# Talking-heads attention on one core: the last 64 keys of the V product in quarters of the array

## The chip, the cores and the metric

One core of one Trainium2 chip. The metric is device time of the whole kernel in microseconds (us): median of the runs. Engines are named as in the profile: PE is TensorE (matmuls), PEld its weight loads, DVE is VectorE, ACT ScalarE, POOL GpSimd, SP SyncE, which issues most transfers.

## The reference

Four batches, 12 heads, 448 positions, head size 64, all float32:

```python
scores = (q @ k.T) / 8                            # per head
scores = einsum('bhij,hg->bgij', scores, w_pre)   # mix heads
attn = exp(scores - max);  attn = attn / (sum(attn) + 1e-9)
attn = einsum('bhij,hg->bgij', attn, w_post)      # mix heads again
x = attn @ v                                      # the V product, (4*448) x 768
```

Two feed-forward layers follow (768 to 2048 to 768 with ELU, 768 to 1024 to 768 with SoLU and a layer norm). The change is in the attention part alone.

## The kernel before

**Work units.** A group is 10 query rows of a batch with all 12 heads. Two groups make a unit, 90 units in all. A chunk is up to 12 groups (120 query rows) of one batch; there are 17 chunks, whose widths add up to 4 x 448 rows. Ten groups' scores lie on partitions as (row, head), so that a head mix is a matmul.

**Stages.** Per chunk, `add_score` (L446) forms the scores of two heads at a time, four 64x64 quarters of the array at once, into two banks of the ring `sc`, which has three; ACT or DVE evacuate them (L452) and a DMA deals them out into the layout (row, head). Per unit, `pre` (L518, tile `pm`) mixes heads, DVE takes the row maximum (L523), ACT the exponential with its sum (L528), DVE and POOL make `wr`, the weights of the second mix divided by the sum. `post` (L551, tile `po`) then multiplies: stationary is a block of 64 keys of `e` (60 partitions x 64 keys), moving is `wr` (60 x 60: 12 heads x 5 rows), so that keys come out on partitions. A unit has two groups (s) of two halves (r, 5 rows each); each quarter of the array has its own (s, x), x being the half of the partitions on which the keys land. 448 keys are 7 blocks of 64: blocks 2q and 2q+1 for q = 0 to 2 fill both halves of 128 partitions, block 6 is the one left over. In `po` its r = 0 rows lie on the lower half and its r = 1 rows on the upper half, the rest of these columns are zeros, set once at the start (L479). `take` (L559) copies each group's `po` (128 x 480) into the chunk's `at` on ACT or DVE. There are two `po` banks, one per group, and both are needed by each unit: a unit's `post` waits for the `take`s of the unit before.

**The V product** (`mm`, L595 to 601, tile `av`) takes a chunk's `at` when all its groups are in: for each half n of the heads (6 heads), 3 head pairs, 4 key pairs q and the two heads k of the pair, 24 matmuls of 128 partitions x 64 stationary columns, two side by side in the array. For q = 3 the array's 128 rows hold block 6 twice (the host's `vt` has it twice), and the zeros in `at` make each row count once. A half is one bank of `sc`, is copied to SBUF (L607) and stored.

A float32 matmul shows as two instructions in the trace, each with a weight load of its own.

**What sets the order.** Nothing is issued in program order here: every stage is an `op` with a rank (a due time in us), resources and planned costs, and `schedule()` (L298) walks them once at build time: it takes the engine that can start first and of its ready operations the one with the lowest rank. `bufs` (L286) holds the rings, among them 3 `sc`, 3 `pm`, 2 `po`. Each engine then runs the order that came out. The ranks come from L363 to 396 with the planned costs `PRE, POST, AV, SC` (L364); a chunk's two V products are due three units after its last `post`.

Of the kernel before, what the change touches and what calls it, by code (L numbers as in the profile page):

```python
# [9 lines left out]
F32 = mybir.dt.float32  # L10
# [54 lines left out]
def kernel(ctx: ExitStack, tc: tile.TileContext, qa, kt, vt, wpre, wpost,  # L65
# [297 lines left out]
    t_pre, t_post, t_av, t_sc = {}, {}, {}, {}  # L363
    PRE, POST, AV, SC, HID = .76, .83, 2.6, .76, 3.64  # L364
    t, nf, t_hid = T0, 0, None
# [10 lines left out]
    for u in range(NU):  # L376
        while nf < min(NU, u + LEAD + 1):
            plan_front()
        t_post[u] = t
        t += POST  # L380
        if pending and u - pending[0][0] == 3:
            for k in pending.pop(0)[1]:
                t_av[k] = t
                t += AV
        for c in range(NC):
            if last_of[c] == u:
                pending.append((u, [(c, 0), (c, 1)]))
        if u + 1 == NU:
            t_hid = t
            t += 2 * HID  # L390
            for i, k in enumerate(sum((k for _, k in pending), [])):
                t_av[k] = t_hid - 1 + i
# [5 lines left out]
    kt_t, kb, q_t, qb_, sp_t, sp_op, pre_op, e_t = {}, {}, {}, {}, {}, {}, {}, {}  # L398
    po_t, ps_t, st_t, wr_t, v_t, x_t, at_t, T = {}, {}, {}, {}, {}, {}, {}, {}
    k_op, q_op, av_op, sc_ev = {}, {}, {}, {}  # L400
# [76 lines left out]

    for t in po_p:
        op(T0 + 2, lambda e, t=t: nc.vector.memset(t, 0.0), dve=.49)  # L479
    o_clear = {c + 3: clear(sp_t[c][:, CH[c][2]:], .38 * (NH - CH[c][2]), 4.0 + c) for c in range(2)}  # L480
# [24 lines left out]
    for u, sl in enumerate(units):  # L505
# [36 lines left out]
        def post(e, u=u, ns=2):  # L542


            ps = po_t[u] = po_p
            for todo in [[(r, 2 * q + x, q, x) for x in range(2)] for r in range(2) for q in range(3)] + [[(0, 6, 3, 0), (1, 6, 3, 1)]]:
                for r, n, q, x in todo:
                    for s in range(ns):
                        sl = slice(64 * s, 64 * s + 60)
                        out = ps[s][64 * x:64 * x + 64, q * 120:q * 120 + 120].rearrange("p (g a) -> p g a", a=10)  # L550
                        nc.tensor.matmul(out[:, :, 5 * r:5 * r + 5], e_t[u, r][sl, 64 * n:64 * n + 64],  # L551
                                         wr_t[u][sl, r].rearrange("p (g a) -> p g a", a=5), start=True, stop=True)

        def take(e, s, u=u, sl=sl):
            c, g = sl[s]
            if c not in at_t:
                at_t[c] = pools["at"].tile([128, 4, NH, WMAX], F32, tag="at", name="at")
            o, n = 10 * g, min(10, width_of(c) - 10 * g)
            copier(e)(at_t[c].rearrange("p q h r -> p (q h) r")[:, :, o:o + n],  # L559
                      po_t[u][s][:, :480].rearrange("p (x a) -> p x a", a=10)[:, :, :n])  # L560

# [11 lines left out]
        for s, (c, g) in enumerate(sl):  # L573
            at_ops[c].append(op(r0 + 1.2 + .1 * s, lambda e, s=s, take=take: take(e, s), [o], [at_b[c]] if g == 0 else [],
                                [pob[s]] + ([at_b[c]] if g else []), act=.45, dve=.57))


    for c in range(NC):
        b = CH[c][0]
        w = width_of(c)  # L580
        if c == HEAD[b]:
# [7 lines left out]
            for i in range(6):  # L589
                ov.append(op(t_av[c, 0] - VD + 4 * i if b else T0 + 8 + 2.5 * i, lambda e, i=i, load=load: load(e, i), [o_begin], [] if i else [vb], [vb] if i else [], sp=.5, lag=4.0))  # L590
        for n in range(2):
            r = t_av[c, n]
            xb, avb = Buf("x"), Buf("sc")

            def mm(e, c=c, n=n, w=w):  # L595
                ps = x_t[c, n] = ps_sc.tile([128, 512], F32, tag="sc", name="av")[:, :3 * w].rearrange("p (k w) -> p k w", k=3)
                for i in range(3):
                    for q in range(4):
                        for k in range(2):
                            nc.tensor.matmul(ps[64 * k:64 * k + 64, i, :], v_t[CH[c][0]][:, 6 * n + 2 * i + k, q, :], at_t[c][:, q, 6 * n + 2 * i + k, :w],  # L600
                                             start=q == 0, stop=q == 3)

            o = op(r, mm, at_ops[c] + ov, [avb], [vb, at_b[c]], pe=AV * w / 120)

            def take(e, c=c, n=n, w=w):
                T["x", c, n] = pools["xt"].tile([128, 3, WMAX], F32, tag="x", name="x")
                copier(e)(T["x", c, n][:, :, :w], x_t[c, n])  # L607

# [4 lines left out]

            o = op(r + AV + .2, take, [o], [xb], [avb], act=.36, dve=.42)
            T["xs", c, n] = op(r + AV + 1, store, [o], [], [xb], sp=.5, more=.2)

# [62 lines left out]
    gln_t = None  # L679
    lc = NC - 1  # L680
    t0 = t_pre[first[lc]]
# [39 lines left out]
    for ft in range(2):  # L721
        o = None
        for p in range(3):
            o = op(t_hid + HD + ft * .01, lambda e, ft=ft, p=p: hid(0, 0, ft, range(2 * p, 2 * p + 2)),
                   need + [o] + [sc_ev[lc, h] for h in range(NH)], pe=HID / 3)
    for i in range(3):
# [253 lines left out]
```

## Time and profile before

| | us |
|---|---|
| median of 3 runs | 1081.91 |
| the runs | 1080.24, 1081.91, 1084.91 |
| span of the profiled execution, first to last instruction | 1077.6 |
| of this, the attention part up to the first matmul of the feed-forward alone | about 358 |

The total of the profiled execution is not listed apart from the three runs; its span stands 4.3 us below their median. Lines of a profile read: start or group, engine, line of the kernel, operation, written tile <- read tiles, shape, count.

### The profile page before, as it was taken

What the parts mean: (1) busy time and instruction counts of PE and PEld (TensorE: products, weight loads), DVE (VectorE), ACT (ScalarE), POOL (GpSimd) and SP (SyncE); (2) the same over time, 40 slices, a digit from 0 to 9 for tenths busy, and PEclk for the clock granted to TensorE, in tenths of its full rate; (3) what the DMA queues carried; (4) which work ended last, traced back from release to release, by engine and by line L of the source; (5) the groups of instructions that cost most, each with busy time, mean ns of one, the idle gap of its engine ahead of it and who ended that gap; (6) DMA issues with size and microseconds to landing.
All of it is one profiled execution on the core that took longest, in us unless ns stands there. A gap on an engine that the chain in (4) does not pass through costs nothing.

```text
span 1077.6 us, 28434 instructions
## 1 busy us (share of the span) xinstructions
PE 1052.9 (98%) x11800; PEld 886.6 (82%) x11800; DVE 719.2 (67%) x1394; ACT 502.4 (47%) x1068; POOL 240.7 (22%) x240
## 2 busy tenths in 40 slices
PE   6899999999999999999999999999999999999998
PEld 2467777677677889998998999999998889898988
DVE  5587776877878566887878887778754734353522
ACT  3476766776776454333433334333331524242422
POOL 4011111111114324353443443433431000000000
PEclk9999999999999999999999999999999999999999
DMA  6776876776746342415161332424272400000001
GB/s 206 205 225 186 238 229 195 230 229 196 227 146 195 98 147 79 155 52 185 58 204 65 123 117 87 148 78 145 71 273 100 163 23 23 23 28 17 30 15 45
DMA packets 80522, 141.69 MB, mean 131 GB/s; under 512 B 20648, under 2 KB 60424, under 8 KB 80392
## 3 DMA queue, kind: packets, MB, share of 16 engines
q1 hardware_dynamic: 78255, 136.45, 39.9%
q10 hardware_dynamic: 2137, 3.41, 1.1%
q8 instruction: 93, 1.52, 0.6%
q14 instruction: 37, 0.30, 0.1%
HBM read 75.96 MB, written 25.17 MB: 94 GB/s over the span
## 4 chain that ended last, share of the span: by engine, by line
PE 78%; DVE 9%; DMA 6%; ACT 3%; issue 3%; SPq 1%; POOL 1%; ACTq 0%; DVEq 0%; POOLq 0%
PE h L258 15%; PE o L753 15%; PE o L896 11%; PE h L849 11%; PE av L600 6%; PE po L551 6%; PE pm L518 6%; PE sc L446 6%; DMA ws<-in_wo_dram 2%; DVE x L769 1%; DMA sp<-sev 1%; DVE wy L186 1%; DMA ws<-in_wi_dram 1%; PE tr L880 1%; DVE wq L182 1%
## 5 line engine op out<-in xcount | busy, mean ns | idle before, releaser
L753 PE MATMUL o<-gh,woh 128*128 128x448 f32 x384 | 141.3, 368 | 3.6 <-ACT x L767 1.9
L528 ACT ACTIVATE e<-pm,st 128x448 f32<-128x448 f32 x180 | 113.6, 636 | 64.1 <-DVE st L523 56.7
L523 DVE TENSOR_REDUCE st<-pm 128x1 f32<-128x448 f32 x180 | 105.6, 617 | 52.6 <-PE pm L518 50.5
L753 PE MATMUL o<-glo,woh 128*128 128x448 f32 x384 | 140.0, 365 | 0.0
L753 PE MATMUL o<-gh,wol 128*128 128x448 f32 x384 | 139.7, 364 | 0.0
L271 POOL TENSOR_TENSOR glo<-g,gh 128x448 fp32r<-128x448 f32 x64 | 84.0, 1312 | 217.8 <-issue 125.1
L551 PEld LDWEIGHTS po<-wr,e 60*64 60x64 f32 x5040 | 100.8, 135 | 36.2 <-issue 21.7
L446 PE MATMUL sc<-kt,q 64*64 64x448 f32 x816 | 119.5, 560 | 8.9 <-DMA kt<-in_kt_dram 4.0
L896 PE MATMUL o<-w,lh 128*128 128x384 f32 x448 | 120.3, 340 | 0.0
L518 PE MATMUL pm<-sp,wpre_t 64*64 64x448 f32 x720 | 108.6, 556 | 5.0 <-ACT e L528 4.2
L551 PE MATMUL po<-wr,e 60*64 60x60 f32 x5040 | 107.1, 219 | 2.7 <-issue 1.8
L849 PE MATMUL h<-w,x2h 128*128 128x512 f32 x336 | 107.7, 395 | 0.0
L769 DVE TENSOR_TENSOR x<-x,o 128x448 f32<-128x448 f32 x168 | 101.4, 610 | 7.9 <-PE o L753 7.9
L258 PE MATMUL h<-xh,wih 128*128 128x448 f32 x288 | 105.6, 367 | 0.0
L258 PE MATMUL h<-xh,wil 128*128 128x448 f32 x288 | 105.1, 365 | 0.0
L258 PE MATMUL h<-xl,wih 128*128 128x448 f32 x288 | 104.8, 364 | 0.0
L266 ACT ACTIVATE t<-t 128x448 f32<-128x448 f32 x64 | 37.0, 578 | 136.1 <-DVE t L265 136.1
L539 POOL TENSOR_TENSOR wr<-wpost_t,st 128x120 f32<-128x120 f32 x88 | 34.1, 388 | 283.8 <-DVE st L535 228.0
L600 PEld LDWEIGHTS av<-at,v 128*64 128x64 f32 x1632 | 75.5, 137 | 15.9 <-issue 6.5
L600 PE MATMUL av<-at,v 128*64 128x120 f32 (+5 forms) x1632 | 82.9, 258 | 1.3 <-issue 0.8
L896 PEld LDWEIGHTS o<-w,lh 128*128 128x128 f32 x448 | 81.7, 188 | 0.6
L753 PEld LDWEIGHTS o<-gh,woh 128*128 128x128 f32 x384 | 72.1, 188 | 11.9 <-DVE x L769 3.9
(96 smaller groups left out, 1936.3 us busy)
## 6 DMA issues: line engine op xcount, KB each, us to landing
sp<-sev SPq DMA_DIRECT2D x93, 210.0 KB
ws<-in_wi_dram SPq DMA_DIRECT2D x33, 512.0 KB
ws<-in_wo_dram SPq DMA_DIRECT2D x21, 512.0 KB
q<-in_qa_dram SPq DMA_DIRECT2D x34, 192.0 KB
v<-in_vt_dram SPq DMA_DIRECT2D x24, 256.0 KB
w2s<-ws SPq DMA_DIRECT2D x12, 512.0 KB
ws<-in_wo_dram SPq DMA_DIRECT2D x16, 384.0 KB
w2s<-ws SPq DMA_DIRECT2D x16, 384.0 KB
```

What stands on the lines that cost most here:

```text
L258: nc.tensor.matmul(ps[:, :S], a[:, kc * FG + ft * 128:kc * FG + (ft + 1) * 128], x[:, kc, :], start=kc == 0 and n == 0, stop=kc == ECH - 1 ...
L271: nc.gpsimd.tensor_tensor(glo, g, f(gh), ALU.subtract)
L446: nc.tensor.matmul(T[key][i][64 * x:64 * x + 64, :S], q[sl, h % 6 // 2, 64 * x:64 * x + 64], k[sl, :], start=True, stop=True)
L518: nc.tensor.matmul(ps_t[u][r][64 * s:64 * s + 64, :S], wpre_t[p, :], sp_t[c][p, g, :], start=True, stop=True)
L523: nc.vector.tensor_reduce(out=st_t[u][:P, r:r + 1], in_=ps_t[u][r][:P, :S], op=ALU.max, axis=AX.X, negate=True)
L528: nc.scalar.activation(out=t[:P], in_=ps_t[u][r][:P, :S], func=AF.Exp, bias=st[:P, r:r + 1], scale=1.0, accum_out=st[:P, 2 + r:3 + r])
L551: nc.tensor.matmul(out[:, :, 5 * r:5 * r + 5], e_t[u, r][sl, 64 * n:64 * n + 64], wr_t[u][sl, r].rearrange("p (g a) -> p g a", a=5), start ...
L600: nc.tensor.matmul(ps[64 * k:64 * k + 64, i, :], v_t[CH[c][0]][:, 6 * n + 2 * i + k, q, :], at_t[c][:, q, 6 * n + 2 * i + k, :w], start=q ...
L753: nc.tensor.matmul(ps[:, :S], a[:, ft * DM + e * 128:ft * DM + (e + 1) * 128], x, start=n == 0, stop=n == 5)
L769: nc.vector.tensor_tensor(x1[tb][:, e, :], x1[tb][:, e, :], ps[:, :S], ALU.add)
L849: nc.tensor.matmul(ps[:, hf * 512:hf * 512 + 512], a[:, k, :], w, start=n == 0, stop=n == 3 * ECH - 1)
L896: nc.tensor.matmul(ps[:, :384], a[:, k, :], w, start=n == 0, stop=n == 3 * FC - 1)
```

## The change

- `post` now spreads block 6 by heads: heads 0 to 5 on the lower half of the partitions, heads 6 to 11 on the upper half, with both r. So block 6 of one r is two matmuls of 30 columns (one per half), where it was one of 60. The columns of `po` go from 480 to 420 and have no zeros; the two clearing operations at the start go.
- `at` is laid out as 84 columns (q, head, r; for block 6 six heads and r) x 60 rows-by-5.
- The V product is two operations per chunk. `whole(0)`: heads 0 to 5, the three full key pairs, 18 matmuls of 128 x 64. Then `both`: `whole(1)` for heads 6 to 11, and `rest`: block 6 of all heads, 12 matmuls of 64 x 64, where heads 0 to 5 use the lower and 6 to 11 the upper rows of the array, two heads side by side: four quarters at a time.
- Both halves' banks are taken before `whole(0)` and read after `both`. They are two of the three `sc` banks, for the last chunk the two `po` banks.
- Planned costs: AV 2.6 twice becomes AV0 2.0 and AV1 2.8; `take` .45/.57 becomes .41/.52. The first hidden products of the feed-forward (`hid`) are now booked on the `sc` ring and behind the V product of the last chunk but one.

```diff
-    PRE, POST, AV, SC, HID = .76, .83, 2.6, .76, 3.64
+    PRE, POST, AV0, AV1, SC, HID = .76, .83, 2.0, 2.8, .76, 3.64
...
-    for t in po_p:
-        op(T0 + 2, lambda e, t=t: nc.vector.memset(t, 0.0), dve=.49)
...
             ps = po_t[u] = po_p
-            for todo in [[(r, 2 * q + x, q, x) for x in range(2)] for r in range(2) for q in range(3)] + [[(0, 6, 3, 0), (1, 6, 3, 1)]]:
-                for r, n, q, x in todo:
-                    for s in range(ns):
-                        sl = slice(64 * s, 64 * s + 60)
-                        out = ps[s][64 * x:64 * x + 64, q * 120:q * 120 + 120].rearrange("p (g a) -> p g a", a=10)
-                        nc.tensor.matmul(out[:, :, 5 * r:5 * r + 5], e_t[u, r][sl, 64 * n:64 * n + 64],
-                                         wr_t[u][sl, r].rearrange("p (g a) -> p g a", a=5), start=True, stop=True)
+            for r in range(2):
+                for n in range(7):
+                    for x in [n % 2] if n < 6 else range(2):
+                        for s in range(ns):
+                            sl = slice(64 * s, 64 * s + 60)
+                            out = ps[s][64 * x:64 * x + 64, :420].rearrange("p (l a) -> p l a", a=5)
+                            w = wr_t[u][sl, r].rearrange("p (g a) -> p g a", a=5)
+                            if n < 6:
+                                out = out[:, 12 * (n - x) + r:12 * (n - x) + 24:2]
+                            else:
+                                out, w = out[:, 72 + r:84:2], w[:, 6 * x:6 * x + 6]
+                            nc.tensor.matmul(out, e_t[u, r][sl, 64 * n:64 * n + 64], w, start=True, stop=True)
...
+        av_of = [Buf("po" if c == lc else "sc") for _ in range(2)]
+        def whole(e, n, c=c, G=G):
+            if n == 0:
+                for m in range(2):
+                    x_f[c, m] = po_p[m] if c == lc else ps_sc.tile([128, 512], F32, tag="sc", name="av")
+            x_t[c, n] = x_f[c, n][:, :30 * G].rearrange("p (k s r a) -> p k r s a", k=3, r=2, a=5)
+            at = at_t[c].rearrange("p l (s a) -> p l s a", a=5)
+            for i in range(3):
+                for q in range(3):
+                    for k in range(2):
+                        h = 6 * n + 2 * i + k
+                        l = 24 * q + 2 * h
+                        nc.tensor.matmul(x_t[c, n][64 * k:64 * k + 64, i], v_t[CH[c][0]][:, h, q, :], at[:, l:l + 2, :G],
+                                         start=i == 0 and q == 0, stop=False, skip_group_check=True)
+        def rest(e, c=c, G=G):
+            at = at_t[c].rearrange("p l (s a) -> p l s a", a=5)
+            for i in range(3):
+                for n in range(2):
+                    for k in range(2):
+                        p, l = slice(64 * n, 64 * n + 64), 72 + 4 * i + 2 * k
+                        nc.tensor.matmul(x_t[c, n][64 * k:64 * k + 64, i], v_t[CH[c][0]][p, 6 * n + 2 * i + k, 3, :], at[p, l:l + 2, :G],
+                                         start=False, stop=True, skip_group_check=True)
...
+        o = op(t_av[c, 0], lambda e, whole=whole: whole(e, 0), at_ops[c] + ov, av_of, [vb, at_b[c]], pe=AV0 * G / 12)
+        o = av_op[c] = op(t_av[c, 1], both, [o], [], [vb, at_b[c]] + av_of, pe=AV1 * G / 12)
```

## Rows read from the trace of the kernel before

**Rows 1.** The page: busy time by engine, and the chain's shares by line.
```profile
PE 1052.9 (98%) x11800; PEld 886.6 (82%) x11800; DVE 719.2 (67%) x1394; ACT 502.4 (47%) x1068; POOL 240.7 (22%) x240
...
PE h L258 15%; PE o L753 15%; PE o L896 11%; PE h L849 11%; PE av L600 6%; PE po L551 6%; PE pm L518 6%; PE sc L446 6%; DMA ws<-in_wo_dram 2%; DVE x L769 1%; DMA sp<-sev 1%; DVE wy L186 1%; DMA ws<-in_wi_dram 1%; PE tr L880 1%; DVE wq L182 1%
```
**Rows 2.** Windows, six stretches that hold a chunk's V products: one, and the sum.
```profile
core 0: us, PE busy (x) PEld busy (x) DVE busy (x) ACT busy (x) POOL busy (x), PEclk, DMA share, GB/s
238.37:248.45 10.08, 10.08 (x244) 7.70 (x241) 5.28 (x14) 5.70 (x16) 0.81 (x3) 1.00 0.66 202
sum 61.93, PE 61.93 PEld 47.43 DVE 34.08 ACT 35.08 POOL 5.31; mean PE 10.32 PEld 7.91 DVE 5.68 ACT 5.85 POOL 0.88
```
**Rows 3.** Windows, six stretches between them: one, and the sum.
```profile
248.45:259.77 11.32, 11.27 (x300) 7.55 (x295) 11.06 (x30) 9.66 (x28) 1.55 (x4) 1.00 0.58 166
sum 69.79, PE 69.63 PEld 46.98 DVE 66.20 ACT 60.15 POOL 9.18; mean PE 11.60 PEld 7.83 DVE 11.03 ACT 10.02 POOL 1.53
```
**Rows 4.** Windows of L551 (`post`) alone, the same two kinds of stretch.
```profile
238.37:248.45 10.08, 1.98 (x112) 2.02 (x112) 1.00 0.66 202
248.45:259.77 11.32, 4.95 (x224) 4.75 (x224) 1.00 0.58 166
```
**Rows 5.** Timeline of PE in one chunk's cycle: start, us, what.
```profile
238.37 2.68 PE L600 MATMUL av<-at,v 128*64 128x120 f32 x48
240.98 0.98 PE L518 MATMUL pm<-sp,wpre_t 64*64 64x448 f32 x8
241.78 0.99 PE L551 MATMUL po<-wr,e 60*64 60x60 f32 x56
242.60 0.94 PE L446 MATMUL sc<-kt,q 64*64 64x448 f32 x8
243.47 2.68 PE L600 MATMUL av<-at,v 128*64 128x120 f32 x48
...
249.95 1.32 PE L551 MATMUL po<-wr,e 60*64 60x60 f32 x56
```
**Rows 6.** Timeline of PE: V product of the narrowest chunk, 40 columns.
```profile
47.00 1.60 PE L600 MATMUL av<-at,v 128*64 128x40 f32 x48
```
**Rows 7.** Groups by shape of PE, 45 to 330 us: busy us, mean ns.
```profile
L551 PE MATMUL po<-wr,e 60*64 60x60 f32 x4480 | 94.5, 219 | 2.2 <-issue 1.8 <-ACT at L559 0.2
L600 PE MATMUL av<-at,v 128*64 128x120 f32 x768 | 42.9, 268 | 0.0
...
L600 PE MATMUL av<-at,v 128*64 128x40 f32 x86 | 2.9, 229 | 0.0
```
**Rows 8.** Waits, 45 to 330 us: us in total, times, longest.
```profile
DVE at L559 <- PE po L551: 8.0, 12, 1.1
...
PEld po L551 <- ACT at L559: 5.7, 23, 0.5
...
ACT at L559 <- PE po L551: 2.6, 6, 0.5
```
**Rows 9.** Groups by shape, 0 to 360 us: the copies of `po`.
```profile
L559 DVE COPY at<-po 128x480 f32<-128x480 f32 x89 | 56.4, 650 | 10.6 <-PE po L551 10.1 <-ACT sev L452 0.2
...
L559 ACT COPY at<-po 128x480 f32<-128x480 f32 x87 | 48.2, 573 | 5.6 <-PE po L551 5.6
...
L559 DVE COPY at<-po 128x384 f32<-128x384 f32 x3 | 1.6, 546 | 0.0
```
**Rows 10.** Timeline of PE at the end of the attention part.
```profile
353.57 2.24 PE L600 MATMUL av<-at,v 128*64 128x98 f32 x48
356.36 2.24 PE L600 MATMUL av<-at,v 128*64 128x98 f32 x48 [0.55 <-ACT x L607]
358.53 0.47 PE L258 MATMUL h<-xh,wih 128*128 128x448 f32 x1
```
**Rows 11.** Timeline of DVE at the start.
```profile
2.84 1.03 DVE L479 MEMSET po<- 128x512 f32 x2
5.90 0.62 DVE L452 COPY s<-sc 128x448 f32<-128x448 f32 x1 [2.04 <-PE sc L446]
```

More of the change, by code (lines that the diff above doesn't have):

```diff
@@ L383 @@
                 t_av[k] = t
-                t += AV
+                t += AV1 if k[1] else AV0
         for c in range(NC):
@@ L398 @@
     kt_t, kb, q_t, qb_, sp_t, sp_op, pre_op, e_t = {}, {}, {}, {}, {}, {}, {}, {}
-    po_t, ps_t, st_t, wr_t, v_t, x_t, at_t, T = {}, {}, {}, {}, {}, {}, {}, {}
+    po_t, ps_t, st_t, wr_t, v_t, x_t, x_f, at_t, T = {}, {}, {}, {}, {}, {}, {}, {}, {}
     k_op, q_op, av_op, sc_ev = {}, {}, {}, {}
@@ L556, in take @@
             if c not in at_t:
[L557 to L560, printed above, removed]
+                at_t[c] = pools["at"].tile([128, 84, WMAX // 2], F32, tag="at", name="at")
+            copier(e)(at_t[c][:, :, 5 * g:5 * g + 5], po_t[u][s][:, :420].rearrange("p (l a) -> p l a", a=5))
         r0 = t_pre[u]
@@ L574 @@
             at_ops[c].append(op(r0 + 1.2 + .1 * s, lambda e, s=s, take=take: take(e, s), [o], [at_b[c]] if g == 0 else [],
-                                [pob[s]] + ([at_b[c]] if g else []), act=.45, dve=.57))
+                                [pob[s]] + ([at_b[c]] if g else []), act=.41, dve=.52))
+    lc = NC - 1
     for c in range(NC):
         b = CH[c][0]
-        w = width_of(c)
+        w, G = width_of(c), CH[c][2]
         if c == HEAD[b]:
@@ L590 @@
                 ov.append(op(t_av[c, 0] - VD + 4 * i if b else T0 + 8 + 2.5 * i, lambda e, i=i, load=load: load(e, i), [o_begin], [] if i else [vb], [vb] if i else [], sp=.5, lag=4.0))
-        for n in range(2):
[L592 to L605, printed above, removed]
+        x_of = [Buf("x") for _ in range(2)]
@@ L606, in take, with both @@
+        def both(e, whole=whole, rest=rest):
+            whole(e, 1)
+            rest(e)
+        o = op(t_av[c, 0], lambda e, whole=whole: whole(e, 0), at_ops[c] + ov, av_of, [vb, at_b[c]], pe=AV0 * G / 12)
+        o = av_op[c] = op(t_av[c, 1], both, [o], [], [vb, at_b[c]] + av_of, pe=AV1 * G / 12)
+        for n in range(2):
+            def take(e, c=c, n=n, G=G):
                 T["x", c, n] = pools["xt"].tile([128, 3, WMAX], F32, tag="x", name="x")
-                copier(e)(T["x", c, n][:, :, :w], x_t[c, n])
+                copier(e)(T["x", c, n][:, :, :10 * G], x_f[c, n][:, :30 * G].rearrange("p (k w) -> p k w", k=3))
@@ L612, in store @@
                 dma(dst.rearrange("(k p) w -> p k w", k=3), T["x", c, n][:, :, :w])
-            o = op(r + AV + .2, take, [o], [xb], [avb], act=.36, dve=.42)
-            T["xs", c, n] = op(r + AV + 1, store, [o], [], [xb], sp=.5, more=.2)
+            o2 = op(t_av[c, 1] + AV1 + .2 + .1 * n, take, [o], [x_of[n]], [av_of[n]], act=.36, dve=.42)
+            T["xs", c, n] = op(t_av[c, 1] + AV1 + 1 + .1 * n, store, [o2], [], [x_of[n]], sp=.5, more=.2)
     last = None
@@ L679 @@
     gln_t = None
-    lc = NC - 1
     t0 = t_pre[first[lc]]
@@ L721 @@
     for ft in range(2):
-        o = None
+        o, hb = None, [Buf("sc")]
         for p in range(3):
             o = op(t_hid + HD + ft * .01, lambda e, ft=ft, p=p: hid(0, 0, ft, range(2 * p, 2 * p + 2)),
-                   need + [o] + [sc_ev[lc, h] for h in range(NH)], pe=HID / 3)
+                   need + [o, av_op[lc - 1]] + [sc_ev[lc, h] for h in range(NH)], [] if p else hb, pe=HID / 3)
     for i in range(3):
```

## The prediction

> **What bounds the kernel now.** The page first: PE is busy 98% of the span, and four attention groups (`av`, `po`, `pm`, `sc`) hold 6% of the chain each [rows 1]. A busy PE is not yet a PE at its peak, so the next question is which engine sets the pace where these four run. The windows split the attention part into two kinds of stretch that follow each other, once per chunk. Where V products stand, PE is busy throughout and DVE and ACT hold 34.08 and 35.08 of 61.93 us, 55% and 57% [rows 2]: PE bounds. Between them DVE holds 66.20 and ACT 60.15 of 69.79 us, 95% and 86% [rows 3]: DVE and ACT bound, and PE waits inside `po`. The count of `po` instructions shows it: 112 (two units of 56) take 1.98 us in the first kind, 0.99 a unit; 224 (four units) take 4.95 in the second, 1.24 a unit [rows 4], and the timeline has one of 1.32 beside one of 0.99 [rows 5]. So a third of the units, 30 of 90, lie where PE bounds, two thirds, 60, where it has about 0.25 us a unit to spare.
>
> The change moves PE work from `av` to `po`. Its result hangs on where each lies.
>
> **V product, removed and added.** A half of 48 instructions takes 2.68 us at 120 columns, the last one's own 0.268 included [rows 5, 7]. Two run side by side, so 24 pairs with 23 steps: (2.68 - 0.268)/23 = 0.105 us a pair. Per chunk the change takes away 6 pairs in each half, 12 in all, -1.26 us. It adds `rest`: 24 instructions in 6 groups of four. A group streams the same 120 columns, so 0.105 each, +0.63. Net -0.63 per full chunk. The widths add up to 1,792 rows, 14.9 full chunks: -9.4. Four chunks now carry two padding columns in 36 pairs, 0.0009 us a column: +0.25. The change between the array's 128-row and 64-row shapes is made as often as before: the one between `whole` and `rest` stands for the one between `av` and the next `pm`. Sum **-9.2 us**, all of it where PE bounds.
>
> **Post, added.** Per unit the columns streamed are the same (60, or 30 twice) but there are 64 instructions for 56, each with a weight load. The price of a short one is shown by the narrowest chunk: its V product streams 40 columns, and a pair takes (1.60 - 0.229)/23 = 0.060 us [rows 6, 7]. `po` streams 60, and a group of four takes (0.99 - 0.219)/13 = 0.059 [rows 5, 7]. A third fewer columns buy nothing, so both stand on a floor per load of 64 columns, and a group of 30 columns stands on it too. Two more groups a unit: +0.119 us. In the 30 units where PE bounds that is **+3.6**.
>
> The Trainium skill has a rule that speaks against the change here ("TensorEngine Tiling (Array Packing)", Instruction Overhead): a matmul of one column takes as long as one of 60, and no tiling factor should be taken from a dimension that is small already. The rows of 40 and 60 columns agree with it. Another of its pages ("TensorE: Matmul & The Clock Gate", LDWEIGHTS) makes a load last as many cycles of 1.2 GHz as it has columns, 53 ns for 64: by that estimate the two groups would cost 0.107 us instead of 0.119, and the term 3.2 instead of 3.6.
>
> **Post where DVE and ACT bound.** In the other 60 units the extra 0.119 fits into the 0.25 us that PE waits there, if what ends the wait does not move with it. Mostly it doesn't: in 80 units with 160 copies of `po`, only 12 on DVE and 6 on ACT found their engine idle and waiting for `po`; the others waited for their turn, and `po`'s own waits are for the copies of the unit before [rows 8]. The copies shrink from 480 to 420 elements: on DVE 480 take 0.650 and 384 take 0.546 [rows 9], 1.08 ns an element, so -0.065 each, one of the two on the busier engine. So between -0.065 (DVE sets the pace and keeps it) and +0.119 (all of it shows) a unit: -3.9 to +7.1 us. The rows on waits lie nearer to the low end; but the order was planned with .83 for a `post` that will take about .93, so every operation behind it comes a little later than planned. I take **0**, for both.
>
> **The ring `sc`.** The V product now holds two of three banks from the start of `whole(0)` until its copies are made, and a score pair needs two: none can run between the halves. Before, one often stood there, 0.87 us up to the next start [rows 5]. Such a pair moves to the second kind of stretch, where its two copies (one each on DVE and ACT) set the price instead of PE. If PE finds `pm` and `po` of the next units instead, this costs nothing or gains the difference of some 0.2 us a chunk, -3; if it finds nothing, up to 0.87 us in each of 15 chunks, +13. I take **0**: the three units planned ahead give PE a `pm` and a `po` for each half, and both engines have 45% to spare there [rows 2]. The copies to SBUF and the stores of the first half come some 5 us later; only the feed-forward reads them.
>
> **The end.** The last chunk's second half waits 0.55 us for the copy of the first [rows 10], since `hid` holds two `sc` banks. In `po` banks it has no such wait: **-0.6**. What is next there is the copies of the last unit, as before.
>
> **The start.** The two clearing operations end at 3.87 us, and DVE then idles 2.04 us for the first scores [rows 11]: **0**, with that idle time as cover; uncovered it would be -1.0.
>
> **Output order.** `whole` writes PSUM in runs of five columns. `po` does so too and stays on its floor, so such a run costs at most what 0.059 for 60 columns allows: 0.119 for a pair of 120 in place of 0.105, on 36 pairs of 14.9 chunks at most +7.5. Below 0 nothing, since the order adds no speed. I take 0: the row of 40 columns written in one run has the same floor.
>
> **Sum:** -9.2 + 3.6 - 0.6 = **-6.2 us**, a span of 1,071.4 for 1,077.6. Outside it nothing changes; the span stands 4.3 us below the median of 1,081.9 (the profiled execution's own total isn't listed), so 1,075.7. A measurement of this kernel can tell about 0.5% from no change, 5.4 us; the line to faster lies at 1,076.5.
>
> **Rivals.**
> - *PE bounds everywhere.* If the copies' waits move with `po`, all 90 loads show: 90 x 0.119 = +10.7, and -9.2 + 10.7 - 0.6 gives 1,082.8, no change. For it: PE's 98%. Against: 0.25 us of waiting per unit. Chance 0.17.
> - *DVE bounds and keeps what it gets.* Then 60 units gain 0.065 and the pace of the second stretch does not see `po`: -6.2 - 3.9 gives 1,071.8. For it: 95% DVE. Against: the late order. Chance 0.14.
> - *Half-width pieces cost half.* The streaming then decides, `po` grows by nothing: -9.2 - 0.6 gives 1,072.1. [...] The 40-column row speaks against it. Chance 0.06.
> - *PE runs dry at the V product, slower.* With two `sc` banks held, PE stands idle at the place of the missing score pair, 0.87 us in each of 15 chunks: -6.2 + 13 gives 1,088.7. It decides from 0.41 us a chunk on (slower at all), and beyond 0.77 us by over 0.5%. For it: in the cycle of rows 5 a score pair stands between the halves. Against: 45% spare on DVE and ACT at that place, so the next unit's inputs are there. Chance 0.18.
> - *The new output order slows PE*, +7.5: 1,083.2. Chance 0.04.
>
> The forecast has 0.41. Its own spread, half of the bounds of the second stretch, is 1,072 to 1,079; two thirds of it lie beyond the line to faster at 1,076.5, 0.28. Faster: 0.28 + 0.14 + 0.06 = 0.48. Same: 0.13 + 0.17 + 0.02 = 0.32. Slower: 0.18 + 0.02 = 0.20. The range for 8 in 10 takes in both faster rivals, the one of no change and part of the slower one: 1,069.5 to 1,086.5.
>
> **What would show it.** Right: `av` with 72 instructions at 0.052 each and 24 at about 0.026; `po` with 64 instructions, 0.94 of its own steps for 0.77; `at` copies of 0.585 on DVE; in stretches with V products PE still full; between them no longer time per unit. Wrong: `po` of 0.99 as before (half-width pieces are cheap), longer stretches between the V products (PE bounds there too), idle PE or late `sc` behind `whole(0)` (the ring).

## The result and the profile after

The changed kernel takes 1,095.0 us in the median (1,092.1 to 1,098.3) against 1,082.1 for the kernel before in the same comparison: a ratio of 1.0119, 95% interval 1.0094 to 1.0144, so **12.9 us slower (10.2 to 15.6)**. The forecast was 1,075.7 with a range of 1,069.5 to 1,086.5. The result lies outside it, on the other side of no change.

The profiled execution of after ran 1,092.1 us with a span of 1,090.3, 12.7 above the span before. The feed-forward's second product (`o`, now L775) starts at 382.73 us for 368.34: all of the loss lies ahead of it, in the attention part. Lines have moved: `sc` L446, `pm` L516, `e` L526, `wr` L537, `post` L555, `take` L561, `whole` L608, `rest` L618, the copy of a half L630.

The page of after, busy time and chain:

```profile
PE 1054.4 (97%) x12520; PEld 894.8 (82%) x12520; DVE 726.0 (67%) x1412; ACT 495.4 (45%) x1047; POOL 238.6 (22%) x241
...
PE o L775 15%; PE h L258 15%; PE o L918 11%; PE h L871 11%; PE po L555 8%; PE pm L516 6%; PE sc L446 6%; PE av L608 5%; DVE x L791 1%; DVE wy L186 1%; DMA sp<-sev 1%; DMA ws<-in_wo_dram 1%; PE tr L902 1%; DVE wq L182 1%; DMA ws<-in_wi_dram 1%
```

PE's busy sum is up by only 1.5 us [rows 1], though 12.7 us were lost. The loss is idle time, and the page alone doesn't say where.

**The prices came out as worked out.** The chain of waits of after, at a chunk of 11 groups without a stall (start, us, what):

```profile
336.32 0.91 PE po L555 x64
337.23 2.00 PE av L608 x36
339.23 0.78 PE av L618 x24
```

PE's timeline of after, a chunk of 120 columns:

```profile
285.40 3.91 PE L608 MATMUL av<-at,v 128*64 128x120 f32 x72
289.24 0.84 PE L618 MATMUL av<-at,v 64*64 64x120 f32 x24
```

Groups by shape of after, 0 to 370 us (busy us, mean ns, idle time before):

```profile
L561 DVE COPY at<-po 128x420 f32<-128x420 f32 x100 | 57.8, 592 | 23.1 <-PE po L555 22.7
...
L561 ACT COPY at<-po 128x420 f32<-128x420 f32 x80 | 44.2, 565 | 13.4 <-PE po L555 13.2
...
L630 DVE COPY x<-av 128x360 f32<-128x360 f32 x9 | 4.8, 531 | 16.7 <-PE av L618 16.7
```

`whole` takes (3.91 - 0.268)/35 = 0.104 us a pair, as before (0.105). `rest` takes 0.84 for its six groups, (0.84 - 0.272)/5 = 0.114 each. A `post` of 64 instructions lasts 0.91 where one of 56 took 0.82 to the next start [rows 5]: +0.09 for 0.119 predicted. The copies of `po` fell to 0.592 on DVE, as read from [rows 9]. What doubled is the idle time before them: 23.1 us on DVE for 10.6 and 13.4 on ACT for 5.6, in each case waiting for `po`.

**Where the time went.** The windows below split 72 units (from the 13th unit's `post` to the 85th's) into 13 stretches, each from the start of a chunk's first V product to the end of its last, and the rest, in both kernels. (The stretches of [rows 2] are longer ones, of two whole units.) Before, the V products' stretches, sum:

```profile
sum 93.86, PE 93.33 PEld 77.60 DVE 52.05 ACT 56.72 POOL 10.45; mean PE 7.18 PEld 5.97 DVE 4.00 ACT 4.36 POOL 0.80
```

Before, the stretches between them, sum:

```profile
sum 161.52, PE 160.08 PEld 103.17 DVE 138.59 ACT 125.50 POOL 17.89; mean PE 11.43 PEld 7.37 DVE 9.90 ACT 8.96 POOL 1.28
```

After, the V products' stretches, two of them and the sum (columns as in [rows 2]):

```profile
190.01:194.71 4.70, 4.70 (x104) 4.50 (x104) 0.59 (x1) 0.60 (x1) 0.00 (x0) 1.00 0.77 236
...
285.40:290.08 4.68, 4.68 (x106) 4.50 (x104) 1.20 (x4) 1.75 (x6) 0.39 (x1) 1.00 0.80 219
...
sum 73.19, PE 73.19 PEld 65.28 DVE 38.76 ACT 32.18 POOL 8.49; mean PE 5.63 PEld 5.02 DVE 2.98 ACT 2.48 POOL 0.65
```

After, the stretches between, one and the sum:

```profile
260.59:285.40 24.81, 21.97 (x577) 12.98 (x569) 18.50 (x45) 15.39 (x39) 1.94 (x5) 1.00 0.77 228
...
sum 194.58, PE 181.39 PEld 121.91 DVE 158.30 ACT 142.49 POOL 19.45; mean PE 12.96 PEld 8.71 DVE 11.31 ACT 10.18 POOL 1.39
```

The V products' stretches shrank by 20.7 us (93.86 to 73.19), and PE does not idle in them at all. The rest grew by 33.1 (161.52 to 194.58), and there PE's idle time rose from 1.44 to 13.19 us. The work of DVE and ACT moved with it: a V product that runs in one piece leaves them little to do (DVE 0.59 and ACT 0.60 us busy of 4.70 in the first row). Their work in those stretches fell by 13.3 and 24.5 us and went into the others. With the share that both together had there before, (138.59 + 125.50)/161.52 = 1.635, the 300.8 us of work that they now have between would take 184.0 us. It takes 194.6. By this estimate 22 of the 33 us are work that moved in and 11 are standstills. The score pairs alone (L446) show the move. Before (first row) they are in 8 of the 13 stretches of V products; after (second row) in none, with 0.07 us reaching in:

```profile
sum 93.86, PE 7.92 PEld 1.96; mean PE 0.61 PEld 0.15
sum 73.19, PE 0.07 PEld 0.00; mean PE 0.01 PEld 0.00
```

How such a standstill looks. PE's timeline of after, 273 to 285 us (start, us, what, idle time before and its releaser):

```profile
275.36 0.93 PE L555 MATMUL po<-wr,e 60*64 60x60 f32 x46
277.58 0.44 PE L555 MATMUL po<-wr,e 60*64 60x60 f32 x16 [1.29 <-issue]
...
281.92 0.60 PE L516 MATMUL pm<-sp,wpre_t 64*64 64x448 f32 x3 [0.75 <-ACT e L526]
...
284.33 1.13 PE L555 MATMUL po<-wr,e 60*64 60x60 f32 x64 [0.69 <-POOL wr L537]
```

DVE in the same time, and at the end of the V product:

```profile
276.39 0.63 DVE L452 COPY sev<-sc 128x448 f32<-128x448 f32 x1 [1.06 <-DMA sp<-sev]
278.15 0.60 DVE L561 COPY at<-po 128x420 f32<-128x420 f32 x1 [1.13 <-PE po L555]
279.18 0.62 DVE L452 COPY sev<-sc 128x448 f32<-128x448 f32 x1 [0.43 <-DMA sp<-sev]
...
290.18 0.53 DVE L630 COPY x<-av 128x360 f32<-128x360 f32 x1 [2.62 <-PE av L618]
```

ACT at the end of the same V product:

```profile
290.12 0.46 ACT L630 COPY x<-av 128x360 f32<-128x360 f32 x1 [2.97 <-PE av L618]
```

All score pairs now stand between V products. Some of their copies to `sev` wait for the transfers that empty `sev`, the next `pm` comes 0.75 us and the next `po` 0.69 us late, and from this unit's `post` to the next one 9 us pass (275.36 to 284.33). Then the V product runs, and DVE and ACT wait for its end. The wait of 1.29 us inside the first `post` is of another kind.

The waits of after, 45 to 340 us (total us, times, longest):

```profile
ACT x L630 <- PE av L618: 20.0, 11, 4.0
DVE at L561 <- PE po L555: 19.7, 31, 2.2
...
DVE x L630 <- PE av L618: 19.0, 11, 4.0
...
ACT at L561 <- PE po L555: 10.9, 14, 2.2
...
DVE sev L452 <- DMA sp<-sev: 4.4, 6, 1.1
```

The copies of `po` waited for PE 12 times on DVE and 6 on ACT before [rows 8]; now 31 and 14 times. DVE's waits for a V product or for the transfer of `sev` have no row at all in the kernel before, where all copies of the V product ran on ACT.

**What PE itself waited for** in the 72 units of after:

```profile
PE po L555 <- issue: 8.1, 11, 1.3
PE po L555 <- POOL wr L537: 1.9, 3, 0.7
PE sc L446 <- issue: 1.3, 1, 1.3
PE pm L516 <- ACT e L526: 1.1, 2, 0.7
PE po L555 <- ACT at L561: 0.4, 2, 0.3
```

And before:

```profile
PE pm L518 <- DMA v<-in_vt_dram: 0.6, 1, 0.6
PE av L600 <- issue: 0.5, 1, 0.5
```

A wait ended by `issue` has no releaser that the profile shows. So only 3.4 of the 12.8 us are waits for another engine. The 11 waits of 8.1 us stand in the middle of a `post`, at instructions with no semaphore to wait for. Counted over PE's records in the order of their start, they lie 2305, 2047, 257, 1280, 255, 257, 256, 511, 1537 and 1792 apart: multiples of 256 to within one. The same holds for all 123 such waits (over 0.15 us, in the same 72 units) of the 20 traces of this case. The page of after has a DMA queue of the kind `instruction` (packets, MB, share; the kernel before has 93 packets there):

```profile
q8 instruction: 98, 1.61, 0.6%
```

That fits a PE that waits for its next block of instructions to arrive, and neither for scores nor for copies; no run tests it. In the eight traces of kernels with 64 instructions a `post` these waits add up to between 5.6 and 15.2 us, 9.4 in the mean; in the twelve with 56, to between 0 and 6.9, 3.7 in the mean. So some of what the extra loads cost may be paid there.

### The profile page after: what moved, and what is told of

Its sections match the earlier page's. It is cut to its first block, busy times and chain, and to the rows that moved or that the text cites. A ratio compares the mean times of both kernels' runs of the same rounds, so it can differ in the third digit from the quotient of the medians.

```text
span 1090.3 us, 29876 instructions
## 1 busy us (share of the span) xinstructions
PE 1054.4 (97%) x12520; PEld 894.8 (82%) x12520; DVE 726.0 (67%) x1412; ACT 495.4 (45%) x1047; POOL 238.6 (22%) x241
## 4 chain that ended last, share of the span: by engine, by line
PE 79%; DVE 9%; DMA 4%; ACT 3%; issue 3%; POOL 1%; SPq 0%; ACTq 0%; DVEq 0%; POOLq 0%
PE o L775 15%; PE h L258 15%; PE o L918 11%; PE h L871 11%; PE po L555 8%; PE pm L516 6%; PE sc L446 6%; PE av L608 5%; DVE x L791 1%; DVE wy L186 1%; DMA sp<-sev 1%; DMA ws<-in_wo_dram 1%; PE tr L902 1%; DVE wq L182 1%; DMA ws<-in_wi_dram 1%
## 5 line engine op out<-in xcount | busy, mean ns | idle before, releaser
L555 PEld LDWEIGHTS po<-wr,e 60*64 60x64 f32 x5760 | 114.7, 135 | 47.2 <-issue 28.6
L526 ACT ACTIVATE e<-pm,st 128x448 f32<-128x448 f32 x180 | 113.7, 636 | 71.0 <-DVE st L521 58.8
L775 PE MATMUL o<-gh,woh 128*128 128x448 f32 x384 | 141.3, 368 | 2.4 <-ACT x L789 1.9
L775 PE MATMUL o<-glo,woh 128*128 128x448 f32 x384 | 140.0, 365 | 0.0
L775 PE MATMUL o<-gh,wol 128*128 128x448 f32 x384 | 139.6, 364 | 0.0
L555 PE MATMUL po<-wr,e 60*64 60x60 f32 (+1 forms) x5760 | 118.3, 218 | 13.8 <-issue 10.8
L446 PE MATMUL sc<-kt,q 64*64 64x448 f32 x816 | 120.3, 564 | 10.3 <-DMA kt<-in_kt_dram 4.3
L516 PE MATMUL pm<-sp,wpre_t 64*64 64x448 f32 x720 | 103.7, 550 | 6.1 <-ACT e L526 3.9
L537 POOL TENSOR_TENSOR wr<-wpost_t,st 128x120 f32<-128x120 f32 x89 | 35.0, 393 | 302.5 <-DVE st L533 229.7
L775 PEld LDWEIGHTS o<-gh,woh 128*128 128x128 f32 x384 | 72.1, 188 | 10.8 <-DVE x L791 2.8
L775 PEld LDWEIGHTS o<-glo,woh 128*128 128x128 f32 x384 | 72.0, 188 | 6.0
L775 PEld LDWEIGHTS o<-gh,wol 128*128 128x128 f32 x384 | 72.1, 188 | 5.5
```

The source lines that it names most:

```text
L446: nc.tensor.matmul(T[key][i][64 * x:64 * x + 64, :S], q[sl, h % 6 // 2, 64 * x:64 * x + 64], k[sl, :], start=True, stop=True)
L516: nc.tensor.matmul(ps_t[u][r][64 * s:64 * s + 64, :S], wpre_t[p, :], sp_t[c][p, g, :], start=True, stop=True)
L526: nc.scalar.activation(out=t[:P], in_=ps_t[u][r][:P, :S], func=AF.Exp, bias=st[:P, r:r + 1], scale=1.0, accum_out=st[:P, 2 + r:3 + r])
L555: nc.tensor.matmul(out, e_t[u, r][sl, 64 * n:64 * n + 64], w, start=True, stop=True)
L775: nc.tensor.matmul(ps[:, :S], a[:, ft * DM + e * 128:ft * DM + (e + 1) * 128], x, start=n == 0, stop=n == 5)
```

## The experiments

Theories: **loads** (the extra loads of `post` cost more than 3.6 us), **hold** (the two held banks cost it), **V product** (its saving doesn't come through), **plan** (planned costs that no longer fit), later **late scores**, **DVE blocked** and **place** (that no score pair can stand in the V product's stretch is the price, and no bank by itself). All us are against the kernel before, as ratio times its median, with the 95% interval in brackets. Each experiment has one profiled execution, which need not be a typical one.

**1. Loads alone** (e1_split), the kernel before with block 6 as two matmuls of 30 columns:

```diff
-                for r, n, q, x in todo:
+                for r, n, q, x, g0, g1 in [(*t, g0, g1) for g0, g1 in ([(0, 12)] if todo[0][1] < 6 else [(0, 6), (6, 12)]) for t in todo]:
...
+                        nc.tensor.matmul(out[:, g0:g1, 5 * r:5 * r + 5], e_t[u, r][sl, 64 * n:64 * n + 64],
+                                         w[:, g0:g1], start=True, stop=True)
```

> The kernel before, only that block 6 of each half r is done as two matmuls of 30 columns (heads 0-5, 6-11) in the same quarter as before: 64 instructions a unit for 56, same result, same plan, same V product. Theory 'loads' (the eight more weight loads of a unit show nearly everywhere, and the waits behind a longer po grow with them): 9 to 13 us above before. Theory 'hold' (the two sc banks held over both halves of the V product keep scores out and make them late): only the units at the V products show, +3 to +5. Theory 'plan' (an order planned with .83 for a post of .93 stalls the engines): +6 to +12, since the plan is just as wrong here.

1,088.6 us, 1.006 [1.0031, 1.0089]: **+6.5 us** (3.4 to 9.6). Of 90 x 0.119 = 10.7 us of PE's work 61% shows, where the forecast let a third show (3.6, still inside the interval). The value lies below the range of the theory of the loads and inside that of the plan, which the third experiment excludes. In its 72 units PE waits 7.0 us without a semaphore, at places multiples of 256 instructions apart, as in after.

**2. Hold alone** (e2_hold), the kernel before with both banks of a chunk's V product taken ahead of its first half and copied out after its second:

```diff
+        avbs = [Buf("sc") for _ in range(2)]
...
-            o = op(r, mm, at_ops[c] + ov, [avb], [vb, at_b[c]], pe=AV * w / 120)
+            o = op(t_av[c, n], mm, at_ops[c] + ov + [o], [] if n else avbs, [vb, at_b[c]] + (avbs if n else []), pe=AV * w / 120)
```

> The kernel before, only that both halves' sc banks are taken before the first half of the V product and copied out after the second. No other instruction differs. Theory 'hold': 8 to 13 us above before. Theories 'loads' and 'plan': within 2 us of before.

1,094.4 us, 1.0105 [1.0052, 1.0158]: **+11.4 us** (5.6 to 17.1), with no instruction added. The order that came out puts 17 of the 34 copies of the V product on DVE, where all were on ACT. The 72 units of this kernel and of the one before in one window each; before:

```profile
77.21:332.59 255.38, 253.40 (x6455) 180.77 (x6448) 190.64 (x492) 182.22 (x487) 28.34 (x73) 1.00 0.71 210
```

With both banks held:

```profile
74.35:344.55 270.20, 259.85 (x6464) 180.38 (x6456) 200.47 (x507) 177.31 (x475) 28.31 (x73) 1.00 0.68 199
```

After:

```profile
76.17:343.94 267.77, 254.58 (x7021) 187.19 (x7016) 197.07 (x502) 174.67 (x465) 27.93 (x72) 1.00 0.67 196
```

PE idles 2.0 us before, 10.4 with the banks held (its busy time is 6.5 us longer there as well, with x6464 instructions for x6455), 13.2 after. Of the waits without a semaphore, multiples of 256 instructions apart, this trace has none.

**3. Plan** (e3_plan: after, e7_plan_only: before), `POST` raised from .83 to .93, about what `post` takes now (0.91). The edit, here in after:

```diff
-    PRE, POST, AV0, AV1, SC, HID = .76, .83, 2.0, 2.8, .76, 3.64
+    PRE, POST, AV0, AV1, SC, HID = .76, .93, 2.0, 2.8, .76, 3.64
```

> The changed kernel with the planned cost of post at .93 instead of .83, nothing else. Theory 'plan': the stalls go, 1077 to 1083 us. Theories 'loads' and 'hold': within 4 us of the changed kernel's 1095.

> The kernel before with the planned cost of post at .93 instead of .83, nothing else: no instruction differs, only their order. A control for what a new order alone does. If the order alone moves the time little: within 3 us of before. If new orders cost some us whatever they are for: 4 to 8 us above before, and then the loads and the hold are overrated by as much.

After with the fitting cost: 1,098.5, 1.0136 [1.0085, 1.0187], no better than after. Before with the unfitting one: 1,083.9, 1.0007 [0.9989, 1.0025]. The theory of the plan falls. The second kernel is also a control for a new order as such. Its 72 units:

```profile
73.58:336.02 262.44, 257.00 (x6455) 179.41 (x6448) 191.95 (x492) 182.77 (x489) 29.13 (x73) 1.00 0.69 206
```

They last 7.1 us longer than before, with 5.4 us of idle PE, though the kernel as a whole is no slower. So a window of the 72 units shows where PE idles in one execution; what a change costs is read from the times.

**4. Saving of the V product** (e5_no6), the kernel before without block 6 in its V product, the plan left as it is:

```diff
-                    for q in range(4):
+                    for q in range(3):
```

> The kernel before with block 6 left out of the V product (q = 0 to 2 alone; the output lacks these 64 keys' share), plan and order unchanged: 12 of 48 pairs less per chunk, twice what the change saves there. Theory 'PE bounds at the V products': 24 pairs... 12 pairs x 0.105 x 14.9 chunks = 18.8 us less, measured 15 to 19 us below before. Theory 'DVE and ACT set the pace over a whole cycle' (what PE is spared at the V product is given back as waits in the next stretch): 3 to 9 us below before.

1,073.5 us, 0.9923 [0.9897, 0.9948]: **-8.3 us** (-11.1 to -5.6). PE's work falls by 12 pairs of 14.9 chunks, 12 x 0.105 x 14.9 = 18.8, so 44% of it comes through (30 to 59%). The window of its 72 units shows the same: PE's busy time falls by 11.7, the stretch by 6.2, and PE now idles 7.5 us.

```profile
74.46:323.66 249.20, 241.75 (x6144) 167.76 (x6136) 190.66 (x492) 181.28 (x487) 28.39 (x73) 0.99 0.73 215
```

**5. Shorter hold in the changed kernel** (e4_rest_first): `rest` first, so that each half is complete, and copied, by itself; and the reverse (e6_one_op), the whole V product as one operation.

```diff
-        o = op(t_av[c, 0], lambda e, whole=whole: whole(e, 0), at_ops[c] + ov, av_of, [vb, at_b[c]], pe=AV0 * G / 12)
-        o = av_op[c] = op(t_av[c, 1], both, [o], [], [vb, at_b[c]] + av_of, pe=AV1 * G / 12)
+        os = [op(t_av[c, 0], both, at_ops[c] + ov, av_of, [vb, at_b[c]], pe=AV0 * G / 12)]
+        os.append(op(t_av[c, 1], lambda e, whole=whole: whole(e, 1), [os[0]], [], [vb, at_b[c], av_of[1]], pe=AV1 * G / 12))
```

> The changed kernel with the quarters of block 6 done first, together with heads 0-5, so that this half's bank is complete and copied out after the first of the two operations, and a score pair can run between them; planned costs 2.8 and 2.0 instead of 2.0 and 2.8. The work is the same. Theory 'hold': 1080 to 1086 us. Theories 'loads' and 'plan': within 3 us of the changed kernel's 1095.

> The changed kernel with the whole V product of a chunk as one operation of PE (about 4.5 us in one go), so the two banks are held for a shorter time and nothing runs between the halves. Theory 'scores kept out' (the length of the hold costs): 3 to 6 us below the changed kernel's 1095. Theory 'DVE and ACT run dry' (while PE does nothing but V product, they have nothing to read): 3 to 8 us above it.

`rest` first: 1,088.8, 1.006 [1.0036, 1.0084], half of the loss is gone with the same arithmetic, though less than the theory of the hold said. One operation: 1,096.4, 1.0107 [1.0064, 1.0151], no different from after, in whose order the V product already runs in one go in 8 of 17 chunks; neither theory's range was met.

**6. First half copied at once** (e8_take_first), kernel 2 with the first half's copy ahead of the second half:

```diff
-            o2 = op(t_av[c, 1] + AV + .2 + .1 * n, take, [o], [xbs[n]], [avbs[n]], act=.36, dve=.42)
+            o2 = op(t_av[c, n] + AV + .2, take, [o if n else o_first], [xbs[n]], [avbs[n]], act=.36, dve=.42)
```

> The kernel with both banks held (second experiment), only that the first half's bank is copied out right after the first half, so a score pair fits between the halves again; both banks are still taken at the start. Theory 'scores kept out': within 4 us of before. Theory 'taking two banks at once' (the start of the V product waits until two of three are free): stays 6 us or more above before.

1,092.3, 1.0075 [1.0051, 1.0098]: +8.1 for +11.4, intervals that overlap. The copy's place is no more than part of it. In the order that came out a score pair stands between the halves in 4 chunks, where it does in 9 in the kernel before, in 3 with `rest` first and in none in kernel 2 and in after.

**7. Late scores** (e9_after_early, e10_before_early, e11_rest_first_early, e12_hold_early): the scores' due times 6 us earlier in after, before, kernel 5 and kernel 2.

```diff
-SCM = 18
+SCM = 24
```

> The changed kernel with all scores of a chunk due 6 us earlier (SCM 24 for 18), nothing else. Theory 'late scores' (with two of three sc banks held over the V product, a chunk's last score pair comes so late that the next chunk's first head mix waits for its transfer): the waits go, 1082 to 1088 us. Theory 'banks' (the ring of three is short of banks whatever the due times, scores cannot come earlier): within 4 us of the changed kernel's 1095.

> The kernel before with the same earlier due times (SCM 24), as the control. Its last issue of a chunk's scores stands 7 to 10 us ahead of the first head mix, so both theories: within 4 us of before.

> The kernel with the quarters of block 6 first (fourth experiment) and the earlier due times. Theory 'late scores': 1078 to 1084 us, which would be no slower than before. Theory 'banks': 1086 to 1092, as without them.

> The kernel before with both banks held (second experiment) and the earlier due times. Theory 'late scores': 1081 to 1086 us, the price of the hold gone. Theory 'banks': 1091 to 1098, as without them.

1.0224 [1.0167, 1.0282], 1.0058 [1.0034, 1.0082], 1.0142 [1.0085, 1.0199] and 1.0129 [1.008, 1.0178]: each is slower than the same kernel with 18 or, for the last, not told apart from it. Earlier due times win nothing back, which speaks against late scores. It doesn't exclude them, since the kernel before slows down by 6.3 us too; why was not followed up.

**8. DVE blocked** (e13_hold_act: kernel 2, e14_after_act: after), the copies of the V product on ACT alone, so that none stands at the head of DVE's order waiting for its end:

```diff
-            o2 = op(t_av[c, 1] + AV + .2 + .1 * n, take, [o], [xbs[n]], [avbs[n]], act=.36, dve=.42)
+            o2 = op(t_av[c, 1] + AV + .2 + .1 * n, take, [o], [xbs[n]], [avbs[n]], act=.36)
```

> The kernel before with both banks held (second experiment, 1094), only that both copies of the V product go on ACT, as all 34 do in the kernel before; there 17 of the 34 went on DVE, which stood idle ahead of them for 22 us in all. Theory 'DVE blocked' (DVE takes its orders in sequence, and a copy that waits for the end of the V product holds up the maxima behind it): 1084 to 1089 us. Theory 'banks' (the scores and the V product share three banks and wait for each other's copies): within 3 us of 1094.

> The changed kernel with both copies of the V product on ACT, nothing else. Theory 'DVE blocked': 1086 to 1091 us. Theory 'banks': within 3 us of the changed kernel's 1095.

1.0186 [1.0159, 1.0212] and 1.0083 [1.0056, 1.0111]: worse than its parent in one, perhaps a little better in the other (+9.0 for +12.9, intervals that overlap). DVE's wait of 19.0 us for the V product is mostly where idle time is booked, and not what causes it.

**9. A bank of its own** (e15_own_bank), the kernel before with two banks for scores and one for the V product (the feed-forward's first products change their banks with it):

```diff
-    bufs = {"sc": 3, "pm": 3, "po": 2, "sev": SB, "e": EB, "wr": WB, "st": 4, "kst": 2, "q": 4,
+    bufs = {"sc": 2, "av": 1, "pm": 3, "po": 2, "sev": SB, "e": EB, "wr": WB, "st": 4, "kst": 2, "q": 4,
```

> The kernel before with the ring of three split: two banks for scores alone, one for the halves of the V product alone (in the feed-forward the first products use two and two banks in turn instead of three and one). Theory 'banks' (before, the scores keep two banks and the V product one, so neither waits for the other's copies; the change breaks that): within 4 us of before. If the third bank helps the scores as well: 5 us or more above before.

1,088.3, 1.0035 [1.0013, 1.0056]: +3.8 us (1.4 to 6.1). Sharing the three banks is worth something. It is not the price of the scores' third bank alone, since here a second half also waits until the first half's bank is copied out.

**10. Halves in one go** (e16_in_one_go), the kernel before with the second half due right behind the first:

```diff
+            t_av[k] = t - 2 * AV + .01
```

> The kernel before, only that the second half of the V product is due right behind the first (0.01 us instead of 2.6), so that nothing need run between them; banks are taken and copied as before. Theory 'place' (what costs is that scores and head mixes no longer stand between the halves, where DVE and ACT have time, whether a bank is held or not): 7 to 13 us above before. Theory 'banks': within 4 us of before.

1,085.3, 1.0022 [0.9998, 1.0046]. This told little: the order that came out still had score pairs between ten pairs of halves, so that the edit did not do what it was for.

**11. The order of the scores alone** (e17_gate, e18_gate_copies), the kernel before, its banks as they were, with a rule for the planner only: no score pair from the start of a chunk's first half to the end of its second, and in the other kernel (the last pair of lines) until both halves are copied out.

```diff
-        o1 = op(r, mm, [k_op[b, h], q_op[c, h // 6]], scb, [qb_[c, h // 6], kb[b, h]], pe=SC)
+        o1 = op(r, mm, [k_op[b, h], q_op[c, h // 6]], scb + [Buf("gate")], [qb_[c, h // 6], kb[b, h]], pe=SC)
...
-            o = op(r, mm, at_ops[c] + ov, [avb], [vb, at_b[c]], pe=AV * w / 120)
+            o = o_half = op(r, mm, at_ops[c] + ov + [o_half], [avb] if n else [avb, gate], [vb, at_b[c]] + ([gate] if n else []), pe=AV * w / 120)
...
-            o = op(r + AV + .2, take, [o], [xb], [avb], act=.36, dve=.42)
+            o = op(r + AV + .2, take, [o], [xb], [avb, gate], act=.36, dve=.42)
```

> The kernel before, with one rule more in the plan: no score pair between the first and the second half of a chunk's V product. Banks are taken one at a time and copied as before; no instruction differs, only the order. Theory 'place' (score pairs moved from between the halves into the stretch where DVE and ACT are full): 7 to 13 us above before. Theory 'banks' (the two banks as such, taken before the first half and free only after the copies): within 4 us of before.

> As the run before this, only that the rule holds from the first half until both halves are copied out, which is what two banks held force, still without holding a bank longer. Theory 'place', widened (the scores' standstill over V product and copies costs, by order alone): 8 to 13 us above before, as the held banks of the second experiment (1094). Theory 'banks': within 4 us of before.

Until the second half ends: 1,087.1, 1.0051 [1.0017, 1.0085], **+5.5 us** (1.8 to 9.2), between the ranges of the two theories. Until the copies are made: 1,092.3, 1.0114 [1.0087, 1.0141], **+12.3 us** (9.4 to 15.3), as much as the held banks cost. No bank is held longer here and no instruction added; a change of order alone costs it, and 33 of the 34 copies of the V product are on ACT. An order of another kind, in the third experiment, cost 0.7. The 72 units with the first rule:

```profile
78.87:340.60 261.73, 254.98 (x6433) 181.44 (x6432) 190.15 (x481) 182.44 (x484) 27.94 (x72) 1.00 0.68 201
```

With the second:

```profile
80.14:347.69 267.55, 253.88 (x6349) 175.60 (x6341) 192.46 (x482) 178.39 (x472) 27.78 (x71) 1.00 0.66 194
```

PE idles 6.8 and 13.7 us. The first window is no longer than that of the control in the third experiment, so it tells nothing by itself. The second has the length of after's (267.6 for 267.8) and its idle time (13.7 for 13.2), but is not the same picture: it holds 12 V products for 13, comes from the slowest of the four executions (1,097.7), and only 5.6 us of its idle time are waits without a semaphore, for 8.1.

## Why the prediction was wrong

**The ring `sc`, sized at 0 (bounds -3 and +13): the step that failed.** Held banks alone cost 11.4 us, and an order that keeps the scores away from the V product and its copies costs 12.3 without any bank held longer, near the upper bound. The prediction let the pairs move "to the second kind of stretch", knew that DVE and ACT bound there, and still took 0 because both had 45% to spare in the first kind. That spare time could not be used: without scores in the V product's stretch DVE and ACT had less to do in it than before (38.76 and 32.18 us for 52.05 and 56.72), not more. The question it asked was whether PE finds other work at the place of the missing pair. PE does (it is busy for 73.19 of 73.19 us there); DVE and ACT don't, and the stretches between grow. That the order costs this much is shown by the times; which waits it acts through is not, since most of PE's idle time in after has no releaser.

**The V product, sized at -9.2.** Its price per instruction was right, "all of it where PE bounds" was not. Kernel 4 took twice that work out and 44% came through. By that share, an estimate, the term is -9.2 x 0.44 = -4.1 (-2.8 to -5.5). A likely reason, not tested apart: making PE shorter where DVE and ACT idle already also takes from them the time in which they could catch up.

**`post`, sized at +3.6.** Two more groups cost 0.09 to 0.10 us a unit, for the 0.119 of [rows 5 to 7], and half-width pieces cost nearly what whole ones do. That agrees with the row of 40 columns and with the rule of the Trainium skill that was cited ("TensorEngine Tiling (Array Packing)", Instruction Overhead). The 0 for the 60 units between the V products is the doubtful part: alone, the loads cost 6.5 us (3.4 to 9.6), so part of them probably shows there, but 3.6 is not excluded.

**The sum.** 6.5 - 4.1 + 11.4 (or 12.3) = 13.8 (or 14.7), or 0.6 less with the term of the end, measured 12.9 (10.2 to 15.6). Against the forecast of -6.2 that is 2.9 from the loads, 5.1 from the V product and 11.4 to 12.3 from the ring. That the parts simply add is assumed; the sum allows it, with intervals of 3 to 6 us on each part, and the middle term is scaled, not measured.

**What was right.** The copies of `po` at 0.59, `whole` at 0.052 an instruction and `rest` near it (0.114 a group for 0.105), no price for the new output order, no price for the start (DVE still waits for the first scores, 3.39 us for 2.04), and the end: PE has no idle time of 0.15 us or more from 351.4 to 382.7 us, so the wait of 0.55 us is gone.

**The rivals.** "PE runs dry at the V product" had the right sign and, at 1,088.7, the nearest time, for a wrong reason: PE is never dry there; it is dry 13.2 us between them. "PE bounds everywhere" let all 10.7 us of the loads show; the 6.5 measured lie between that and the 3.6 of the forecast. Those of free half-width pieces and of a dear output order fall with the prices above. That DVE keeps what it gets falls too: it got 0.058 us a copy, and waits longer for `po`.

**What stays open.** How the price of the order divides between DVE and ACT standing in the V products, the transfers out of `sev`, and PE's waits at every 256th instruction or a multiple of that; why these waits are so much longer in after than before; and why earlier due times hurt every kernel but perhaps one. A kernel that splits block 6 by rows, as before, and still does it in quarters was not tried. No complete version here beats the kernel before; the nearest of the changed ones is `rest` first, at 1.006.

## What to carry to other kernels

Where one kind of stretch is bound by PE and the next by the engines that empty its banks, PE's work in the first is also the time in which the others catch up: count what a shorter or more compact stretch leaves them to do, not only what PE saves. A buffer held longer in a shared ring is a change of order for everyone else in that ring, and is tested most cheaply by giving the old kernel that order alone. Price each part with a kernel of its own before adding terms of either sign: here the prices per instruction were right within a quarter, the ring was taken at 0 from a spare time that nothing could use, and the sum was wrong by 19 us. And before a cause is named for PE's idle time, look at what ended each wait: a row with `issue` points at none of the other engines.

## What the hardware showed beyond that

SP is taken for some four fifths of the time, and no busy row says so, since issuing instructions aren't counted. Its timeline before has one transfer `sp<-sev` after another, one every 0.8 to 1.1 us; added up over the 72 units, the rows of its timeline last 210 of 255.4 us (132.9 of the 161.5 between the V products), and 211 of 267.8 after (162.5 of 194.6). A row joins issues less than 0.15 us apart; the issue instructions by themselves last 191 us in each kernel. So between V products SP's rows take 82 and 84% in the two kernels, while their share in the V products' stretches falls from 82 to 66%. That fits the waits of `sev` for its transfers above; whether SP's rate is what lengthens these stretches was not tested.
